# Sliding-window attention and an ELU layer on one core: the score products of a head pair on shared rows

## The chip, the cores and the metric

One core of one Trainium2 chip. The metric is the device time of one execution in microseconds. Three runs of the kernel before took 627.19, 627.75 and 628.57 us; the median is 627.75 us.

## What is computed

Attention over 4 batches, 8 heads, 768 positions and a head dimension of 64, in which a query sees the first 4 keys ("sinks") and the last 128 keys up to its own position; then a layer of 512 -> 2048 -> 512 with an ELU between, on the 3072 rows that come out. All inputs and the output are float32.

```
scores = (q @ k.T) / sqrt(64)
keep   = (key < n_sink) | ((rel >= 0) & (rel < window))     # rel = query - key
a      = softmax(where(keep, scores, -1e9))
x      = (a @ v), heads side by side                        # 3072 x 512
h      = x @ w_in                                           # 512 x 2048
out    = where(h > 0, h, exp(min(h, 0)) - 1) @ w_out        # 2048 x 512
```

## The kernel before

The 3072 rows are 24 tiles of 128 positions, six to a batch. They are worked on in nine chunks of 2, 2, 2, 3, 3, 3, 3, 3 and 3 tiles (`SIZES`). For every chunk there is attention, for 4 head pairs and each tile, and then the layer, for 16 blocks of 128 hidden columns. A tile that is the first of its batch has one block of keys (4 sinks and 128 keys, 132 columns), every other one two blocks (264 columns).

Full precision is had by splitting a float32 operand into two fp16 parts, "hi" and "lo", and summing products of the parts. In the layer (lines 765 and 793) there are three products for each operand pair: hi x hi, hi x lo and lo x hi. The first product of the layer (L765) makes 12 matrix products of 256 or 384 columns a block, the second (L793) three for each tile, of 512 columns. These two lines are most of TensorE's work.

The scores of chunks 0 to 2 (`c < DUP`) are fp32 products of 64 rows: the two heads of a pair lie in rows 0 to 63 and 64 to 127 of one tile, and line 601 issues one product for each, an fp32 product being two instructions. From chunk 3 on the key and query columns of each head are loaded twice, into rows 0 to 63 and again into rows 64 to 127, by `layouts` on the host's side and one load per head (line 523). `split_keys` (line 508) then makes for each head:

- `hi`, by a ScalarE copy to fp16 of all rows (L524),
- `lo` of the keys, all rows, by a VectorE subtraction (L525),
- `lo` of the queries, written over the lower half of `hi`'s query columns (L526).

A product over all 128 rows with these queries as weights hence sums the query's hi and lo parts by itself, and a head's scores take two products: with `hi` (L595) and with `lo` (L596) of the keys. Each head is a task of its own on TensorE, with its own bank of PSUM out of two. VectorE then adds the mask and finds the row's minimum (L616), ScalarE takes the exponential (L618), the probabilities are split into fp16 parts (L668, L669), transposed by a DMA (L687) and multiplied with the values (L701, L706). The value products have 64 columns of weights, head 0 in the left half of the array and head 1 in the right. From chunk 3 on the value products of three tiles are made in one visit.

All instructions are tasks of a planner (`Plan`). A task has an engine, an expected duration, what it depends on, and for TensorE a position in the stream of layer products. `ring` makes the writer of a buffer wait for the users of its former contents; there are two raw key buffers (`kqs`), three split ones (`kq`) and two score banks (`s`). `forward` (line 193) simulates the engines, and each engine's order comes out of it and is then fixed by `keep_order` (line 920). Until 100 us into the plan, small idle products (L882) fill TensorE's holes. `HINTS` (line 891) places branch hints so many tasks before each queue's end. `check_kq` (line 842) loads the keys and queries of chunks 3 to 8 a second time late in the run, to test their range; it takes rows 0 to 63 of one head and 64 to 127 of the other, as two loads.

Of the kernel before, what the change touches and what calls it, by code (L numbers as in the profile page):

```python
# [20 lines left out]
P = 128  # L21
# [28 lines left out]
DUP = 3  # L50
# [18 lines left out]
for _c, _ch in enumerate(CHUNKS):  # L69
    for _p in range(NP):  # L70
        for _e in range(2):
            KQ_OFF[_c, 2 * _p + _e] = KQ_COLS
            if _c >= DUP or _e:
                KQ_COLS += len(key_tiles(_ch)) * KW + len(_ch) * P
KQ_MAX = max(len(key_tiles(c)) * KW + len(c) * P for c in CHUNKS)
KL_MAX = max(len(key_tiles(c)) * KW for c in CHUNKS)
# [289 lines left out]
def fast_path(tc, ctx, first, kq, vx, wt, out, low, spread, numbers, flag):  # L366
# [14 lines left out]
    kqr = rows("kq", [P, KQ_MAX + KL_MAX], F16)  # L381
# [113 lines left out]
    def attention(c):  # L495
# [12 lines left out]
        def split_keys(h):  # L508


            st = kqs[slot("kqs")]
            o, kw = KQ_OFF[c, h], kc + qc
            if c < DUP:
                ld = None
                if (c, h) not in first["kq"]:
                    ld = add("SP", 0.4, lambda: nc.sync.dma_start(st[:, :kw], kq[:, o : o + kw]), lat=dma_us(P * kw * 4) * 1.15)
                users = []
                return st, None, ld, ld, users
            buf = kqr[slot("kq")]
            raw, hi, lo = st[:, :kw], buf[:, :kw], buf[:, KQ_MAX : KQ_MAX + kc]  # L520
            ld = None
            if (c, h) not in first["kq"]:
                ld = add("SP", 0.4, lambda: nc.sync.dma_start(raw, kq[:, o : o + kw]), lat=dma_us(P * kw * 4) * 1.15)
            th = add("ACT", act_us(kw), lambda: nc.scalar.activation(hi, raw, AF.Copy, scale=Q_SCALE), deps=[ld])  # L524
            tk = add("DVE", 0.13 + 0.00108 * kc, lambda: nc.vector.scalar_tensor_tensor(lo, raw[:, :kc], Q_SCALE, hi[:, :kc], ALU.mult, ALU.subtract), deps=[th], slow=1.5)  # L525
            tq = add("DVE", 0.13 + 0.00108 * qc, lambda: nc.vector.scalar_tensor_tensor(hi[D:, kc:], raw[D:, kc:], Q_SCALE, hi[D:, kc:], ALU.mult, ALU.subtract), deps=[th], slow=1.5)  # L526
            users = []
            ring("kqs", [ld or th], [th, tk, tq])
            ring("kq", [th], users)
            return hi, lo, tk, tq, users  # L530
# [39 lines left out]
        for p in range(NP):  # L570
            kqp = [split_keys(2 * p + e) for e in range(2 if c >= DUP else 1)]
# [4 lines left out]
            for g in ts:  # L576
# [13 lines left out]
                def scores(es_, sps=sps, qo=qo, c0=c0, wd=wd, kqp=kqp):  # L590
                    def run():
                        if c >= DUP:
                            hi, lo = kqp[es_[0]][:2]
                            sp, q = sps[es_[0]], hi[:, qo : qo + P]
                            nc.tensor.matmul(sp[:, :wd], q, hi[:, c0 : c0 + wd], start=True, stop=False)  # L595
                            nc.tensor.matmul(sp[:, :wd], q, lo[:, c0 : c0 + wd], start=False, stop=True)  # L596
                            return
                        both = kqp[0][0]
                        for e in es_:
                            r = slice(e * D, (e + 1) * D)  # L600
                            nc.tensor.matmul(sps[e][:, :wd], both[r, qo : qo + P], both[r, c0 : c0 + wd], start=True, stop=True)  # L601
                    return run

                if c >= DUP:
                    scs = [add("PE", 0.225 if nb == 2 else 0.2, scores([e]), deps=kqp[e][2:4], pos=at[k] + 0.01 * e, line=1) for e in range(2)]
                else:
                    scs = [add("PE", 0.65, scores([0, 1]), deps=kqp[0][2:4], pos=at[k], line=1)] * 2
                for kk, sc_ in zip(kqp, scs):
                    kk[4].append(sc_)
                if c < DUP and j == 0:  # L610
                    ring("kqs", [kqp[0][2] or scs[0]], kqp[0][4])
                to_score = -0.125 / (Q_SCALE * Q_SCALE) if c >= DUP else -0.125
                exps, st_users = [], []
                for e in range(2):
                    ee, me = e3[:, e, :wd], mn[:, e : e + 1]
                    red = add("DVE", 0.24 + 0.001 * wd, lambda ee=ee, me=me, sp=sps[e], m=m, wd=wd, to_score=to_score: nc.vector.tensor_tensor_reduce(ee, sp[:, :wd], m[:, :wd], to_score, 3.0e38, ALU.add, ALU.min, me), deps=[scs[e], (None, second_)[t] if t < 2 else rest_])  # L616
                    ring("s", [scs[e]], [red])
# [224 lines left out]
    def check_kq(c, p, k, after):  # L842
        t, n = vm[slot("vm")].rearrange("p a w -> p (a w)"), len(key_tiles(CHUNKS[c])) * KW + SIZES[c] * P

        def both_heads():
            for e in range(2):
                r, o = slice(e * D, (e + 1) * D), KQ_OFF[c, 2 * p + e]
                nc.sync.dma_start(t[r, :n], kq[r, o : o + n])

        ld = add("SP", 0.8, both_heads, deps=[after], lat=2.0 + dma_us(P * n * 4))  # L850
# [6 lines left out]
    for i in range((len(SIZES) - DUP) * NP):  # L857
        check_kq(DUP + i // NP, i % NP, len(SIZES) * NP + i, exps_done[NF * 6 - 4 + 2 * i])
# [32 lines left out]
HINTS = dict(PE=8, ACT=110, DVE=120, SP=50)  # L891
# [50 lines left out]
def general_path(tc, ctx, kq, vx, wt, out, nw):  # L942
# [50 lines left out]
    for b in range(B):  # L993
        x = sb.tile([P, ND, S], F32, name=f"g_x{b}", tag="g_x", bufs=1)
        for h in range(H):
# [3 lines left out]
            for c, ch in enumerate(CHUNKS):  # L999
                kts = key_tiles(ch)  # L1000
                for i, g in enumerate(ch):
# [4 lines left out]
                    r = slice(0, D) if c >= DUP else slice(h % 2 * D, (h % 2 + 1) * D)  # L1006
# [52 lines left out]
def layouts(q, k, v):  # L1059
# [15 lines left out]
    for c, ch in enumerate(CHUNKS):  # L1075
        kts = key_tiles(ch)
        for h in range(H):
            e = h % 2
            o = KQ_OFF[c, h]
            for src, tiles in ((kx, kts), (qT, ch)):  # L1080
                for g in tiles:
                    w = src.shape[4]
                    for r in (0, 1) if c >= DUP else (e,):
                        kq[r * D : (r + 1) * D, o : o + w] = src[g // NT, h, :, g % NT]
# [87 lines left out]
```

## Time and profile before

| | |
|---|---|
| median of three runs | 627.75 us |
| the profiled execution | 628.19 us |
| its span, first to last instruction | 626.3 us |
| TensorE busy with products | 606.1 us |
| TensorE's mean granted clock | 0.991 of full speed |
| DMA moved | 98.24 MB |

The span is counted from the first instruction of the program to the last; what lies around it, 1.9 us, belongs to the time of the execution. Products on TensorE are pipelined: one is on record until its last result is written, while the next has long begun. The time that a product takes from the stream is therefore read from the start of one to the start of the next, not from its duration. A weight load (PEld) overlaps with products.

### The profile page before, as it was taken

What the parts mean: (1) busy time and instruction counts of PE and PEld (TensorE: products, weight loads), DVE (VectorE), ACT (ScalarE), POOL (GpSimd) and SP (SyncE); (2) the same over time, 40 slices, a digit from 0 to 9 for tenths busy, and PEclk for the clock granted to TensorE, in tenths of its full rate; (3) what the DMA queues carried; (4) which work ended last, traced back from release to release, by engine and by line L of the source; (5) the groups of instructions that cost most, each with busy time, mean ns of one, the idle gap of its engine ahead of it and who ended that gap; (6) DMA issues with size and microseconds to landing.
All of it is one profiled execution on the core that took longest, in us unless ns stands there. A gap on an engine that the chain in (4) does not pass through costs nothing.

```text
span 626.3 us, 13397 instructions
## 1 busy us (share of the span) xinstructions
PE 606.1 (97%) x4504; PEld 359.4 (57%) x4504; DVE 462.3 (74%) x1206; ACT 421.2 (67%) x1192; POOL 294.7 (47%) x595
## 2 busy tenths in 40 slices
PE   6997999999999999999999999999999999999995
PEld 4664665667675555555555555555555555555552
DVE  7877677979878786688788988788877887543323
ACT  5887888879878876676667666676767666432221
POOL 4876689875445444344344445334324444222221
PEclk9898999999999999999999999999999999999998
DMA  8698977758656665586456865676655864413101
GB/s 293 210 248 199 298 243 192 209 139 223 145 127 157 162 146 103 94 216 181 125 153 177 230 139 159 130 197 136 166 125 124 209 144 107 115 50 92 55 2 53
DMA packets 122077, 98.24 MB, mean 157 GB/s; under 512 B 98324, under 2 KB 98324, under 8 KB 122004
## 3 DMA queue, kind: packets, MB, share of 16 engines
q1 hardware_dynamic: 122004, 97.34, 60.7%
q8 instruction: 37, 0.61, 0.4%
q14 instruction: 36, 0.29, 0.2%
HBM read 66.38 MB, written 7.34 MB: 118 GB/s over the span
## 4 chain that ended last, share of the span: by engine, by line
PE 91%; POOL 3%; DVE 2%; issue 2%; DMA 1%; ACT 1%; POOLq 0%; ACTq 0%
PE acc L793 39%; PE h L765 38%; PE po L701 5%; PE s L595 2%; PE s L596 2%; PE s L601 2%; POOL w L457 1%; PE h L882 1%; PE acc L636 1%; DMA pt<-pq 1%; DMA vs<-in_vx_dram 1%; PE po L706 1%; PE po L653 0%; DVE pt L334 0%; POOL pq L630 0%
## 5 line engine op out<-in xcount | busy, mean ns | idle before, releaser
L765 PE MATMUL h<-x,w 128*128 128x384 f16 (+1 forms) x1728 | 274.9, 309 | 2.4 <-DVE g L776 2.3
L765 PEld LDWEIGHTS <-w 128*128 128x128 f16 x1728 | 168.3, 98 | 94.8 <-issue 3.2
L786 POOL TENSOR_TENSOR gl<-g,gh 128x384 f16<-128x384 f32 (+1 forms) x144 | 128.7, 894 | 157.3 <-ACT gh L779 134.2
L793 PE MATMUL acc<-w,gh 128*128 128x512 f16 x768 | 192.7, 379 | 1.0 <-POOL w L457 1.0
L773 ACT ACTIVATE g<-h 128x384 f32<-128x384 f32 (+1 forms) x144 | 65.1, 452 | 101.8 <-PE h L765 92.2
L793 PEld LDWEIGHTS <-gh 128*128 128x128 f16 x768 | 72.9, 98 | 69.4 <-issue 0.9
L793 PE MATMUL acc<-w,gl 128*128 128x512 f16 x384 | 109.2, 379 | 0.0
L669 DVE SCALAR_TENSOR_TENSOR pq<-e,st,pq 128x256 f16<-128x256 f32 (+1 forms) x176 | 95.1, 571 | 13.0 <-ACT pq L668 12.7
L618 ACT ACTIVATE e<-e,st 128x264 f32<-128x264 f32 (+1 forms) x192 | 92.9, 484 | 12.2 <-DVE st L616 11.2
L779 ACT ACTIVATE gh<-g 128x384 f16<-128x384 f32 (+1 forms) x144 | 69.3, 481 | 43.2 <-DVE g L776 41.5
L616 DVE CUSTOM_DVE_ANT_0 e<-s,m 128x264 f32<-128x264 f32 (+1 forms) x192 | 71.7, 405 | 26.2 <-PE s L596 19.8
L776 DVE SCALAR_TENSOR_TENSOR g<-g,h 128x384 f32<-128x384 f32 (+1 forms) x144 | 72.8, 506 | 13.2 <-POOL g L775 11.3
L668 ACT ACTIVATE pq<-e,st 128x256 f16<-128x256 f32 (+1 forms) x176 | 77.1, 482 | 5.3 <-DVE st L623 4.1
L775 POOL TENSOR_SCALAR g<-g 128x384 f32<-128x384 f32 (+1 forms) x80 | 41.5, 518 | 80.2 <-ACT g L773 79.8
L775 DVE TENSOR_SCALAR g<-g 128x384 f32<-128x384 f32 (+1 forms) x64 | 26.8, 419 | 65.7 <-ACT g L773 65.4
L793 PEld LDWEIGHTS <-gl 128*128 128x128 f16 x384 | 37.5, 98 | 46.6 <-POOL gl L786 0.9
L524 ACT ACTIVATE kq<-kqs 128x780 f16<-128x780 f32 (+1 forms) x48 | 42.7, 901 | 15.7 <-PE s L596 12.2
L457 POOL TENSOR_TENSOR w<-wv,w 128x256 f16<-128x256 f32 x64 | 49.2, 789 | 5.4 <-ACT w L456 4.7
L622 POOL TENSOR_SCALAR st<-st 128x2 f32<-128x2 f32 x84 | 21.2, 253 | 48.0 <-ACT e L618 44.1
L701 PE MATMUL po<-pt,vh 128*64 128x128 f16 x656 | 35.8, 221 | 2.6 <-DVE x L740 1.9
L618 ACT ACTIVATION_READ_ACCUMULATOR e<-e,st 128x1 f32 x192 | 36.1, 188 | 0.0
L595 PE MATMUL s<-kq 128*128 128x264 f16 (+1 forms) x144 | 34.3, 267 | 0.6 <-ACT x L739 0.6
(92 smaller groups left out, 628.8 us busy)
## 6 DMA issues: line engine op xcount, KB each, us to landing
raw<-in_wt_dram SPq DMA_DIRECT2D x32, 512.0 KB, 4.8
kqs<-in_kq_dram SPq DMA_DIRECT2D x24, 456.0 KB, 3.6
kqs<-in_kq_dram SPq DMA_DIRECT2D x24, 390.0 KB, 3.6
vs<-in_vx_dram SPq DMA_DIRECT2D x28, 256.0 KB, 3.6
out_dram<-wv SPq DMA_DIRECT2D x24, 256.0 KB, 2.6
vm<-in_kq_dram SPq DMA_DIRECT2D x24, 228.0 KB, 3.7
vm<-in_kq_dram SPq DMA_DIRECT2D x24, 195.0 KB, 3.4
vm<-in_vx_dram SPq DMA_DIRECT2D x6, 768.0 KB, 5.3
```

Source lines behind the costliest of these rows:

```text
L616: red = add("DVE", 0.24 + 0.001 * wd, lambda ee=ee, me=me, sp=sps[e], m=m, wd=wd, to_score=to_score: nc.vector.tensor_tensor_reduce(ee, sp ...
L618: ex = add("ACT", 0.47 + 0.00085 * wd, lambda ee=ee, me=me, rs=rs[:, e : e + 1]: nc.scalar.activation(ee, ee, AF.Exp, bias=me, scale=-1.0, ...
L668: a = add("ACT", act_us(nb * P, True), lambda src=src, hi=hi, re=re: nc.scalar.activation(hi, src, AF.Copy, scale=re), deps=[rr])
L669: b = add("DVE", 0.478 if nb == 2 else 0.33, lambda src=src, hi=hi, lo=lo, re=re: nc.vector.scalar_tensor_tensor(lo, src, re, hi, ALU.mult ...
L701: nc.tensor.matmul(po[e * D : (e + 1) * D, oc], vts[i][x][:, vo : vo + D], pt[:, (2 * e + part) * nb + i, :], start=new, stop=last)
L765: nc.tensor.matmul(hp[:, :n], win[:, part, d, :], xx[:, :n], start=k == 0, stop=k == 3 * ND - 1)
L773: a = add("ACT", act_us(n) + 0.18, lambda gf=gf, hp=hp, sums=sums: nc.scalar.activation(gf, hp[:, :n], AF.Exp, scale=1.0 / G_SCALE, accum_ ...
L775: b = add("DVE", 0.14 + 0.00057 * n, lambda gf=gf: nc.vector.tensor_scalar(gf, gf, -1.0, G_SCALE, ALU.add, ALU.mult), deps=[a], slow=2.1, ...
L776: b = add("DVE", dve_us(n), lambda gf=gf, hp=hp: nc.vector.scalar_tensor_tensor(gf, gf, 0.0, hp[:, :n], ALU.min, ALU.max), deps=[b])
L779: th = add("ACT", act_us(n), lambda gf=gf, gh=gh: nc.scalar.activation(gh[:, :n], gf, AF.Copy), deps=[b])
L786: tls.append(add("POOL", pool_us(cut), lambda gl=gl, gf=gf, gh=gh, cut=cut: nc.gpsimd.tensor_tensor(gl[:, :cut], gf[:, :cut], gh[:, :cut], ...
L793: nc.tensor.matmul(acc[i], gg[:, i * P : (i + 1) * P], wout[:, part, :], start=f == f0 and k == 0, stop=f == f1 - 1 and k == 2)
```

## The change

From chunk 3 on the two heads of a pair are no longer loaded twice over all rows; they share one tile as in the first chunks, head 0 in rows 0 to 63 and head 1 in rows 64 to 127. `split_keys` is called once for a pair. `lo` gets a place of its own for the queries too. The scores are three products of 64 rows for each head, hi x hi, hi x lo and lo x hi (query x key), the two heads in turn, and are one task. The product of the two lo parts, which was part of the sum before, is left out. `check_kq` makes one load of 128 rows. Two branch hints move. Cut to its core:

```diff
--- before.py
+++ after.py
...
     for _p in range(NP):
         for _e in range(2):
             KQ_OFF[_c, 2 * _p + _e] = KQ_COLS
-            if _c >= DUP or _e:
+            if _e:
                 KQ_COLS += len(key_tiles(_ch)) * KW + len(_ch) * P
 KQ_MAX = max(len(key_tiles(c)) * KW + len(c) * P for c in CHUNKS)
-KL_MAX = max(len(key_tiles(c)) * KW for c in CHUNKS)
 VT = NP * P
 SINKS = B * NT * VT
 TOK_MAX = max(SIZES) * P
...
 
     kqs = first["kqs"]
     vs = first["vs"]
-    kqr = rows("kq", [P, KQ_MAX + KL_MAX], F16)
+    kqr = rows("kq", [P, 2 * KQ_MAX], F16)
     vh = rows("vh", [P, VT], F16, RINGS["vt"])
     vl = rows("vl", [P, VT], F16, RINGS["vt"])
     sks = rows("sk", [P, VT], F16)
...
                 users = []
                 return st, None, ld, ld, users
             buf = kqr[slot("kq")]
-            raw, hi, lo = st[:, :kw], buf[:, :kw], buf[:, KQ_MAX : KQ_MAX + kc]
+            raw, hi, lo = st[:, :kw], buf[:, :kw], buf[:, KQ_MAX : KQ_MAX + kw]
             ld = None
             if (c, h) not in first["kq"]:
                 ld = add("SP", 0.4, lambda: nc.sync.dma_start(raw, kq[:, o : o + kw]), lat=dma_us(P * kw * 4) * 1.15)
             th = add("ACT", act_us(kw), lambda: nc.scalar.activation(hi, raw, AF.Copy, scale=Q_SCALE), deps=[ld])
-            tk = add("DVE", 0.13 + 0.00108 * kc, lambda: nc.vector.scalar_tensor_tensor(lo, raw[:, :kc], Q_SCALE, hi[:, :kc], ALU.mult, ALU.subtract), deps=[th], slow=1.5)
-            tq = add("DVE", 0.13 + 0.00108 * qc, lambda: nc.vector.scalar_tensor_tensor(hi[D:, kc:], raw[D:, kc:], Q_SCALE, hi[D:, kc:], ALU.mult, ALU.subtract), deps=[th], slow=1.5)
+            tk = add("DVE", 0.13 + 0.00108 * kc, lambda: nc.vector.scalar_tensor_tensor(lo[:, :kc], raw[:, :kc], Q_SCALE, hi[:, :kc], ALU.mult, ALU.subtract), deps=[th], slow=1.5)
+            tq = add("DVE", 0.13 + 0.00108 * qc, lambda: nc.vector.scalar_tensor_tensor(lo[:, kc:], raw[:, kc:], Q_SCALE, hi[:, kc:], ALU.mult, ALU.subtract), deps=[th], slow=1.5)
             users = []
             ring("kqs", [ld or th], [th, tk, tq])
             ring("kq", [th], users)
...
 
         k = 0
         for p in range(NP):
-            kqp = [split_keys(2 * p + e) for e in range(2 if c >= DUP else 1)]
+            kqp = split_keys(2 * p)
 
 
             po = po_ps[slot("po")]
...
                 pq = pqs[slot("pq")]
                 pt = pts[slot("pt")]
 
-                def scores(es_, sps=sps, qo=qo, c0=c0, wd=wd, kqp=kqp):
-                    def run():
-                        if c >= DUP:
-                            hi, lo = kqp[es_[0]][:2]
-                            sp, q = sps[es_[0]], hi[:, qo : qo + P]
-                            nc.tensor.matmul(sp[:, :wd], q, hi[:, c0 : c0 + wd], start=True, stop=False)
-                            nc.tensor.matmul(sp[:, :wd], q, lo[:, c0 : c0 + wd], start=False, stop=True)
-                            return
-                        both = kqp[0][0]
-                        for e in es_:
+                def scores(sps=sps, qo=qo, c0=c0, wd=wd, kqp=kqp):
+                    hi, lo = kqp[:2]
+                    qs, ks = slice(qo, qo + P), slice(c0, c0 + wd)
+                    products = ((hi, hi), (hi, lo), (lo, hi)) if c >= DUP else ((hi, hi),)
+                    for n, (q, k) in enumerate(products):
+                        for e in range(2):
                             r = slice(e * D, (e + 1) * D)
-                            nc.tensor.matmul(sps[e][:, :wd], both[r, qo : qo + P], both[r, c0 : c0 + wd], start=True, stop=True)
-                    return run
-
-                if c >= DUP:
-                    scs = [add("PE", 0.225 if nb == 2 else 0.2, scores([e]), deps=kqp[e][2:4], pos=at[k] + 0.01 * e, line=1) for e in range(2)]
-                else:
-                    scs = [add("PE", 0.65, scores([0, 1]), deps=kqp[0][2:4], pos=at[k], line=1)] * 2
-                for kk, sc_ in zip(kqp, scs):
-                    kk[4].append(sc_)
+                            nc.tensor.matmul(sps[e][:, :wd], q[r, qs], k[r, ks], start=n == 0, stop=n == len(products) - 1)
+
+                sc = add("PE", (0.40 if nb == 2 else 0.30) if c >= DUP else 0.65, scores, deps=kqp[2:4], pos=at[k], line=1)
+                kqp[4].append(sc)
                 if c < DUP and j == 0:
-                    ring("kqs", [kqp[0][2] or scs[0]], kqp[0][4])
+                    ring("kqs", [kqp[2] or sc], kqp[4])
                 to_score = -0.125 / (Q_SCALE * Q_SCALE) if c >= DUP else -0.125
                 exps, st_users = [], []
                 for e in range(2):
                     ee, me = e3[:, e, :wd], mn[:, e : e + 1]
-                    red = add("DVE", 0.24 + 0.001 * wd, lambda ee=ee, me=me, sp=sps[e], m=m, wd=wd, to_score=to_score: nc.vector.tensor_tensor_reduce(ee, sp[:, :wd], m[:, :wd], to_score, 3.0e38, ALU.add, ALU.min, me), deps=[scs[e], (None, second_)[t] if t < 2 else rest_])
-                    ring("s", [scs[e]], [red])
+                    red = add("DVE", 0.24 + 0.001 * wd, lambda ee=ee, me=me, sp=sps[e], m=m, wd=wd, to_score=to_score: nc.vector.tensor_tensor_reduce(ee, sp[:, :wd], m[:, :wd], to_score, 3.0e38, ALU.add, ALU.min, me), deps=[sc, (None, second_)[t] if t < 2 else rest_])
+                    ring("s", [sc], [red])
...
                     exps.append((red, ex))
 
...
     def check_kq(c, p, k, after):
         t, n = vm[slot("vm")].rearrange("p a w -> p (a w)"), len(key_tiles(CHUNKS[c])) * KW + SIZES[c] * P
 
-        def both_heads():
-            for e in range(2):
-                r, o = slice(e * D, (e + 1) * D), KQ_OFF[c, 2 * p + e]
-                nc.sync.dma_start(t[r, :n], kq[r, o : o + n])
-
-        ld = add("SP", 0.8, both_heads, deps=[after], lat=2.0 + dma_us(P * n * 4))
+        o = KQ_OFF[c, 2 * p]
+        ld = add("SP", 0.4, lambda: nc.sync.dma_start(t[:, :n], kq[:, o : o + n]), deps=[after], lat=2.0 + dma_us(P * n * 4))
...
         ring("vm", [ld], new)
         seen.extend(new)
...
     for c in range(len(SIZES)):
         check_v(c, exps_done[NF * 4 + 3 * c])
     for i in range((len(SIZES) - DUP) * NP):
-        check_kq(DUP + i // NP, i % NP, len(SIZES) * NP + i, exps_done[NF * 6 - 4 + 2 * i])
+        check_kq(DUP + i // NP, i % NP, len(SIZES) * NP + i, exps_done[len(exps_done) - 4 - 2 * ((len(SIZES) - DUP) * NP - i)])
 
     def in_range():
         for r, most in ((es_of, EXP_MAX), (v_top, V_MAX)):
...
 VERBOSE = False
 
 
-HINTS = dict(PE=8, ACT=110, DVE=120, SP=50)
+HINTS = dict(PE=8, ACT=90, DVE=120, SP=27)
 E = mybir.EngineType
 QUEUES = dict(PE=E.PE, ACT=E.Activation, DVE=E.DVE, SP=E.SP)
 
...
                         continue
                     j, ts = kts.index(g), slice(g % NT * P, (g % NT + 1) * P)
                     o = KQ_OFF[c, h]
-                    r = slice(0, D) if c >= DUP else slice(h % 2 * D, (h % 2 + 1) * D)
+                    r = slice(h % 2 * D, (h % 2 + 1) * D)
                     nc.sync.dma_start(kt[:, ts], kq[r, o + j * KW + NS : o + (j + 1) * KW])
                     o += len(kts) * KW + i * P
                     nc.sync.dma_start(qt[:, ts], kq[r, o : o + P])
...
             for src, tiles in ((kx, kts), (qT, ch)):
                 for g in tiles:
                     w = src.shape[4]
-                    for r in (0, 1) if c >= DUP else (e,):
-                        kq[r * D : (r + 1) * D, o : o + w] = src[g // NT, h, :, g % NT]
+                    kq[e * D : (e + 1) * D, o : o + w] = src[g // NT, h, :, g % NT]
                     o += w
     return kq, vx
 
```

## Rows read from the trace of the kernel before

**Rows 1.** the page's first part: busy time, share of the span, instructions by engine.

```profile
PE 606.1 (97%) x4504; PEld 359.4 (57%) x4504; DVE 462.3 (74%) x1206; ACT 421.2 (67%) x1192; POOL 294.7 (47%) x595
```

**Rows 2.** the page's fourth part: chain that ended last, shares by engine.

```profile
PE 91%; POOL 3%; DVE 2%; issue 2%; DMA 1%; ACT 1%; POOLq 0%; ACTq 0%
```

**Rows 3.** stretches: length, busy PE, PEld, DVE, ACT, POOL, then PEclk, DMA share, GB/s.

```profile
0.00:120.00 120.00, 106.86 (x826) 69.20 (x827) 91.31 (x260) 96.50 (x269) 88.72 (x183) 0.97 0.82 242
120.00:560.00 440.00, 439.43 (x3362) 259.31 (x3360) 347.05 (x895) 307.53 (x880) 192.06 (x397) 1.00 0.62 148
```

**Rows 4.** waits of PE from 120 us to the end: total us, times, longest.

```profile
PE s L595 <- ACT x L739: 0.6, 1, 0.6
```

**Rows 5.** timeline of PE, a long and a short tile's scores: start us, us.

```profile
300.57 0.28 PE L595 MATMUL s<-kq 128*128 128x264 f16 x1
300.69 0.28 PE L596 MATMUL s<-kq 128*128 128x264 f16 x1
...
301.02 2.11 PE L765 MATMUL h<-x,w 128*128 128x384 f16 x12
302.98 1.46 PE L793 MATMUL acc<-w,gh 128*128 128x512 f16 x6
...
304.92 0.22 PE L595 MATMUL s<-kq 128*128 128x132 f16 x1
...
305.15 2.11 PE L765 MATMUL h<-x,w 128*128 128x384 f16 x12
```

**Rows 6.** score tile: instructions, ns min/median/max, first and last start us, forms.

```profile
L595 PE MATMUL s<-kq x144: 218/276/287, 132.1 to 536.2; 128*128 128x264 f16 x120, 128*128 128x132 f16 x24
L596 PE MATMUL s<-kq x144: 219/276/276, 132.2 to 536.3; 128*128 128x264 f16 x120, 128*128 128x132 f16 x24
L601 PE MATMUL s<-kqs x96: 272/462/806, 5.0 to 110.5; 64*128 64x264 f32 x80, 64*128 64x132 f32 x16
```

**Rows 7.** timeline of PE, a values visit and what stands around it.

```profile
313.38 2.11 PE L765 MATMUL h<-x,w 128*128 128x384 f16 x12
315.43 0.25 PE L701 MATMUL po<-pt,vh 128*64 128x128 f16 x2
315.50 0.22 PE L701 MATMUL po<-pt,vl 128*64 128x128 f16 x2
315.56 0.33 PE L701 MATMUL po<-pt,vh 128*64 128x128 f16 x6
315.73 0.28 PE L701 MATMUL po<-pt,vl 128*64 128x128 f16 x4
...
316.29 0.22 PE L706 MATMUL po<-pt,sk 128*64 128x128 f16 x2
316.44 1.47 PE L793 MATMUL acc<-w,gh 128*128 128x512 f16 x6
```

**Rows 8.** timeline of PE in narrow stretches, the fp32 scores at 91.6 us.

```profile
91.09 0.59 PE L793 MATMUL acc<-w,gl 128*128 128x512 f16 x2
91.62 0.49 PE L601 MATMUL s<-kqs 64*128 64x264 f32 x2
91.94 0.39 PE L601 MATMUL s<-kqs 64*128 64x264 f32 x2
92.26 0.50 PE L765 MATMUL h<-x,w 128*128 128x256 f16 x3
```

**Rows 9.** timeline of PE, scores right behind a values visit.

```profile
427.15 0.22 PE L706 MATMUL po<-pt,sk 128*64 128x128 f16 x2
427.30 0.29 PE L595 MATMUL s<-kq 128*128 128x264 f16 x1
```

**Rows 10.** the page's fifth part: count, busy us, mean ns, idle before, releaser.

```profile
L616 DVE CUSTOM_DVE_ANT_0 e<-s,m 128x264 f32<-128x264 f32 (+1 forms) x192 | 71.7, 405 | 26.2 <-PE s L596 19.8
...
L524 ACT ACTIVATE kq<-kqs 128x780 f16<-128x780 f32 (+1 forms) x48 | 42.7, 901 | 15.7 <-PE s L596 12.2
```

**Rows 11.** timeline of PEld, a weight load of the scores.

```profile
300.58 0.10 PEld L596 LDWEIGHTS <-kq 128*128 128x128 f16 x1
```

## The prediction

> **What bounds the kernel now.** I read the share of each engine first: TensorE 97%, the next engine 74% [rows 1]. The chain of work that ended last says the same, 91% of the span on TensorE [rows 2]. Then I asked where TensorE still has room. Between 120 and 560 us, where all of the changed products lie, it is busy for all but 0.6 us, at a granted clock of 1.00, the 2.4 GHz level; the only wait in the list from there on is one of 0.6 us. Before 120 us some 13 us stand without a product [rows 3, 4]. The scores of chunks 3 to 8, the ones the change rewrites, are four products of 128 rows per tile of a head pair. They slot into the stream without a gap: from 300.57 to 301.02 for 264 columns, 0.45 us, and from 304.92 to 305.15 for 132 columns, 0.23 us [rows 5]. So one long product is 0.1125 us and one short one 0.0575 us. The two lines of the code have 120 long and 24 short instructions each [rows 6]: 60 long and 12 short tiles of a pair, 29.8 us of TensorE. So only what the change does to TensorE's own stream can move the time; work taken off the other engines has no waiting product to release.
>
> **Part 1, the products.** Four products of 128 rows become three rounds of two 64-row products, the heads in different halves of the array. If the halves run together a round takes what one product takes: 3 x 0.1125 = 0.34 us long, 3 x 0.0575 = 0.17 short. That they can is shown by the fp32 scores of the first chunks, which have this very form: two 64-row instructions, 0.46 us the median of one, are over in 0.49 us together [rows 6, 8]. I add 0.01 us for the lag of the second head. In columns alone, this saves 60 x 0.1125 + 12 x 0.0575 = 7.4 us.
>
> **Part 2, entering and leaving the split array.** The trace shows no fp16 64-row product, so its price comes from two neighbours. The nearest in type is the fp16 values visit, which splits the array by columns. Twelve layer products take 1.96 us when more full-array products follow (301.02 to 302.98) and 2.05 us when a visit follows (313.38 to 315.43): 0.09 us to enter [rows 5, 7]. The first pair is followed by the next after 0.07 us, later pairs after 0.055 (315.56 to 315.73 for three): about 0.02 for weights that nothing hides. Leaving, the last pair at 316.29 is followed by a layer product at 316.44: 0.15 instead of 0.055, so 0.095 us; the six products behind it then take 1.47 instead of 1.46, another 0.01 [rows 5, 7]. Together 0.215, say 0.22 us per visit.
>
> The nearest in form is the fp32 score at 91.6 us. Two layer products from 91.09 would end at 91.52 (0.215 each); the scores begin at 91.62, again 0.09 to 0.10 later. Its last round at 91.94 is followed at 92.26, 0.32 later. If 0.095 of that is leaving, a round is 0.225, just twice the fp16 product of the same width. The first round, 91.62 to 91.94, then holds 0.10 of weight loading, and the whole passage costs 0.74 - 0.45 = 0.29 us over its columns [rows 8]. The same gap of 0.09 stands in rows of both kinds of split, so I take it for a cost of the split and not of the type. For the weights I take the fp16 price: 0.22 a passage. The upper end is 0.29. The lower end, the two empty stretches alone, is 0.185; below that only the case that no such stretch occurs, a rival below.
>
> Per tile of a pair: long, 0.22 + 0.01 + 0.34 = 0.57 against 0.45, **+0.12 us**; short, 0.22 + 0.01 + 0.17 = 0.40 against 0.23, **+0.17 us**. That is 60 x 0.1175 + 12 x 0.1725 = 9.1 us. Where scores stand beside a values visit one entry is shared: such neighbours occur six times in the timeline from 120 us on, and I quote one [rows 9]; 6 x 0.1 = 0.6 us back. Sum **+8.5 us**.
>
> **Part 3, the splitting of keys and queries.** One load, one ScalarE copy and two VectorE subtractions per head become one each per pair: 24 fewer of each kind, and 24 fewer loads on SyncE's queue with half the bytes. ScalarE loses half of 42.7 us of copies [rows 10]; the subtractions of VectorE are of the same number. I cost all of it at nothing: both engines already wait for TensorE at this place (the copy 12.2 us in all, the score reduction 19.8 us) [rows 10], while TensorE waits 0.6 us. On SyncE's queue the transposes and loads behind get more room, which again nobody on TensorE is waiting for. If the splits are what that one wait hangs on, the 0.6 us is all there is to win; and as the work shrinks, nothing that it covers is laid open.
>
> **Part 4, both heads in one task.** The six products wait for both score banks and both subtractions, where each head waited for its own before. Behind them on TensorE stand the layer products. VectorE waits for these scores rather than the other way (19.8 us) and the next tile comes 4 us later (300.57, 304.92) [rows 5, 10], so I take nothing. A missed bank would cost up to one reduction, 0.41 us [rows 10]; a few such would be within my range. The first reduction starts some 0.3 us later; its engine has that room.
>
> **Part 5, order and end.** The planner is told 0.40 and 0.30 us for scores it used to count at 0.45 and 0.40, and fewer tasks elsewhere; every queue's order may shift. From 120 to 560 us nothing waits, so that is free; before 120 us, 13 us stand open [rows 3], but the first of the changed scores comes at 132.1 us [rows 6]; a different order of the work ahead could give or take perhaps a tenth, 1.3 us either way. The range checks of the keys become one load of 128 rows instead of two of 64, the same bytes; their trigger works out to the same place in the list of exponentials. The branch hints move, for ScalarE and SyncE only; the trace doesn't show their price, bounded by the 1.9 us around the span (628.19 - 626.3) as gain or loss; I take nothing, as the last products and stores are the same.
>
> **The sum.** The profiled execution took 628.19 us, 0.44 over the median of 627.75. 628.2 + 8.5 = 636.7 in its terms, **636.3 us** as a median. A measurement here can tell about 0.2%, 1.3 us, from no change.
>
> **Rivals.** (A) *Faster: fp16 halves of rows need no emptying of the array.* The drains in fp32 would then belong to fp32 and those of the visits to columns. The time is 628.2 - 7.4 + 72 x 0.01 = 621.5, median 621.1. The point from which it decides: below 0.09 us a passage the change gains. For it: no row shows the new form. Against: fp32 scores and fp16 visits, different in type and in split, show the same 0.09 on entering. The Trainium skill (TensorEngine Tiling (Array Packing), Theoretical Speedup) promises up to twice the speed for a dimension of 64 or less, which by itself gives this rival's time. The same page (Key Properties) says that changing the tiling mode drains the engine, and the two gaps in the rows agree with that.
>
> (B) *The heads take turns.* An fp32 round takes twice the time for the same columns (0.225 against 0.1125), so the halves may share something that fp16 at full rate exhausts. Three more rounds a tile: 60 x 0.34 + 12 x 0.17 = 22.4 us more, 658.7. Against it: the fp16 visits run their pairs together, 0.055 a pair where a product of 132 columns takes 0.0575 [rows 5, 7].
>
> (C) *Weights wait for their own rows.* If a head's next weights could not be loaded while its half streams, rounds two and three would each show a load, 0.10 us by the row of one [rows 11]: 72 x 2 x 0.10 = 14.4 us more, 650.7. Against it: with all 128 rows in use, the load at 300.58 lies inside the product that started at 300.57, and the next starts at 300.69 without a gap [rows 5, 11]; and in fp32 the second round shows no further gap. The Trainium skill (TensorE: Matmul & The Clock Gate, Part 3, The mechanism) says that a weight load overlaps a running product only where the row groups differ, which would give this rival's time; the rows of the full array contradict it as it stands there.
>
> (D) *No net change:* passages at about 0.09 us, half-hidden, 627 to 629.
>
> **Chances.** Forecast 0.78, A 0.10, B 0.05, C 0.04, D 0.03. The number is the forecast's. The range takes the overhead from 0.185 (-2.5 us) to 0.29 (+5.0), the shared entries from none to twice six (0.6 either way) and 1.3 us either way for the order: 636.3 - 4.4 is 631.9 with all three, 636.3 + 5.6 is 641.9 with the first two; I give 631.5 to 642, leaving out A, B, C and D, about 0.2. Faster 0.10 (A), same 0.03 (D), slower 0.87.
>
> **What would show it.** Right: score instructions on 64 rows, two starting together, rounds 0.11 us apart; about 0.09 us between the last layer product's normal end and the first score, and again behind it; a long tile taking 0.57 us of the stream; TensorE still without waits from 120 us; the key copy's count at 24 and its wait gone, with no effect on time. Wrong: a layer product following the third round at 0.11 us (A), six evenly spaced starts (B), rounds at 0.21 us (C), or new waits of TensorE for score banks or keys (part 4).

## The result, and the profile after

The kernel after took 634.64 us (median of four runs, 634.41 to 636.12) against 627.48 us before (four runs as well, one more than the three given above): 1.0116 times as long, with an interval of 1.0096 to 1.0136. That is 7.2 us slower, where 8.5 were forecast; 634.64 lies within the range. The profiled execution took 636.12 us, the longest of the four.

The page's first part and its fourth, of the kernel after, to be held against [rows 1] and [rows 2]:

```profile
PE 613.3 (97%) x4648; PEld 342.0 (54%) x4648; DVE 434.0 (68%) x1164; ACT 404.6 (64%) x1164; POOL 287.9 (45%) x593
...
PE 91%; POOL 4%; DMA 2%; DVE 1%; ACT 1%; issue 1%; SPq 0%; ACTq 0%; POOLq 0%
```

VectorE has 28 us less to do and ScalarE 17, as the change has it, and the time grew all the same: TensorE is still at 97% and holds 91% of the chain. From 120 us to the end the list of TensorE's waits has no entry at all, and the stretches (columns as in [rows 3]) show it busy throughout:

```profile
120.00:560.00 440.00, 440.00 (x3472) 239.09 (x3471) 317.10 (x851) 290.01 (x848) 185.12 (x395) 1.00 0.53 126
```

So the list shows no wait for another engine that could be the loss. The loss stands in the stream of products, and the timeline shows where. One long tile and one short tile of the kernel after; the rows of one and two instructions come from narrow stretches around their starts:

```profile
303.87 0.59 PE L783 MATMUL acc<-w,gl 128*128 128x512 f16 x2
304.39 0.29 PE L596 MATMUL s<-kq 64*128 64x264 f16 x2
304.52 0.39 PE L596 MATMUL s<-kq 64*128 64x264 f16 x4
304.84 0.50 PE L755 MATMUL h<-x,w 128*128 128x384 f16 x2
...
308.53 0.38 PE L783 MATMUL acc<-w,gl 128*128 128x512 f16 x1
308.84 0.23 PE L596 MATMUL s<-kq 64*128 64x132 f16 x2
...
309.12 2.12 PE L755 MATMUL h<-x,w 128*128 128x384 f16 x12
```

The two layer products that start at 303.87 would be done with the stream at 304.30 (0.215 each: six are on record for 1.46 us [rows 5] and one for 0.38); the scores start at 304.39. The first two score instructions take 0.29 us together, from the start of the one to the end of the other, where one alone takes 0.28: they run side by side. The second round starts 0.13 later at 304.52, and the next layer product at 304.84, 0.32 after the second round. Two rounds at 0.1125 are 0.225 of that, and the rest, 0.095, is a gap in which no product starts. The long tile takes 304.84 - 304.30 = 0.54 us of the stream, against 0.45 before [rows 5] and 0.57 forecast. The short one takes 309.12 - 308.75 = 0.37, against 0.23 and 0.40.

The groups of other engines that answer to [rows 10]:

```profile
L606 DVE CUSTOM_DVE_ANT_0 e<-s,m 128x264 f32<-128x264 f32 (+1 forms) x192 | 71.6, 406 | 50.4 <-PE s L596 48.0
...
L523 ACT ACTIVATE kq<-kqs 128x780 f16<-128x780 f32 (+1 forms) x24 | 21.7, 905 | 17.4 <-PE s L596 17.4
```

The copies went from 48 to 24, and work that was saved turned into longer waits for TensorE: 48.0 us in front of the score reduction instead of 19.8, 17.4 in front of half as many copies instead of 12.2.

### The profile page after: what moved, and what is told of

Read it like the earlier page. It is cut to its first block, busy times and chain, and to the rows that moved or that the text cites. A ratio compares the mean times of both kernels' runs of the same rounds, so it can differ in the third digit from the quotient of the medians.

```text
span 634.3 us, 13457 instructions
## 1 busy us (share of the span) xinstructions
PE 613.3 (97%) x4648; PEld 342.0 (54%) x4648; DVE 434.0 (68%) x1164; ACT 404.6 (64%) x1164; POOL 287.9 (45%) x593
## 4 chain that ended last, share of the span: by engine, by line
PE 91%; POOL 4%; DMA 2%; DVE 1%; ACT 1%; issue 1%; SPq 0%; ACTq 0%; POOLq 0%
PE acc L783 39%; PE h L755 39%; PE s L596 6%; PE po L691 5%; POOL w L456 2%; DMA raw<-in_wt_dram 2%; PE po L696 1%; PE h L868 1%; POOL pq L620 1%; DVE pt L333 0%; ACT wu L306 0%; POOL gl L776 0%; ACT pq L658 0%; ACT g L763 0%; DVE pq L659 0%
## 5 line engine op out<-in xcount | busy, mean ns | idle before, releaser
L755 PEld LDWEIGHTS <-w 128*128 128x128 f16 x1728 | 164.8, 98 | 103.4 <-issue 10.4
L776 POOL TENSOR_TENSOR gl<-g,gh 128x384 f16<-128x384 f32 (+1 forms) x144 | 126.2, 877 | 170.1 <-ACT gh L769 140.9
L783 PEld LDWEIGHTS <-gh 128*128 128x128 f16 x768 | 71.1, 98 | 74.5 <-issue 6.6
L765 DVE TENSOR_SCALAR g<-g 128x384 f32<-128x384 f32 (+1 forms) x70 | 28.4, 405 | 69.4 <-ACT g L763 69.3
L765 POOL TENSOR_SCALAR g<-g 128x384 f32<-128x384 f32 (+1 forms) x74 | 37.2, 503 | 59.0 <-ACT g L763 58.5
L596 PE MATMUL s<-kq 64*128 64x264 f16 (+1 forms) x432 | 34.8, 267 | 0.0
L691 PEld LDWEIGHTS <-vh 128*64 128x64 f16 x656 | 26.6, 111 | 13.7 <-issue 13.6
```

The source lines that it names most:

```text
L596: nc.tensor.matmul(sps[e][:, :wd], q[r, qs], k[r, ks], start=n == 0, stop=n == len(products) - 1)
L691: nc.tensor.matmul(po[e * D : (e + 1) * D, oc], vts[i][x][:, vo : vo + D], pt[:, (2 * e + part) * nb + i, :], start=new, stop=last)
L755: nc.tensor.matmul(hp[:, :n], win[:, part, d, :], xx[:, :n], start=k == 0, stop=k == 3 * ND - 1)
L765: b = add("DVE", 0.14 + 0.00057 * n, lambda gf=gf: nc.vector.tensor_scalar(gf, gf, -1.0, G_SCALE, ALU.add, ALU.mult), deps=[a], slow=2.1, ...
L776: tls.append(add("POOL", pool_us(cut), lambda gl=gl, gf=gf, gh=gh, cut=cut: nc.gpsimd.tensor_tensor(gl[:, :cut], gf[:, :cut], gh[:, :cut], ...
L783: nc.tensor.matmul(acc[i], gg[:, i * P : (i + 1) * P], wout[:, part, :], start=f == f0 and k == 0, stop=f == f1 - 1 and k == 2)
```

## The experiments

To keep the start out of the comparison I also read one stretch in every trace: from the first product of the layer's second half for chunk 3 (the fourth chunk) to that for chunk 7, four chunks of work. In it lie 48 score tiles of head pairs, 40 long and 8 short, and 16 values visits; the layer's products are the same in every kernel. Its length in the kernel before, from the two products that bound it in the timeline of TensorE (line numbers move with the edits):

```profile
202.96 1.24 PE L793 MATMUL acc<-w,gh 128*128 128x512 f16 x5
...
492.08 1.24 PE L793 MATMUL acc<-w,gh 128*128 128x512 f16 x5
```

The same two products in the kernel after:

```profile
205.11 1.25 PE L783 MATMUL acc<-w,gh 128*128 128x512 f16 x5
...
499.37 1.25 PE L783 MATMUL acc<-w,gh 128*128 128x512 f16 x5
```

289.12 us became 294.26: 5.14 us for 48 tiles, 0.107 us a tile. Seventy-two such tiles make 7.7 us, about the whole of what was measured.

The theory was that each passage into and out of the split array costs about 0.21 us and outweighs the columns saved. Its rivals: that the loss comes from the shared task, the order or the start; that the halves do not run together; and that the work taken off the other engines matters after all.

### No split at all

```diff
+                    if c >= DUP:
+                        for e, k, first_, last_ in ((0, hi, True, False), (0, lo, False, True), (1, hi, True, True)):
+                            nc.tensor.matmul(sps[e][:, :wd], hi[:, qs], k[:, ks], start=first_, stop=last_)
+                        return
                     for n, (q, k) in enumerate(products):
```

> The kernel after, but from chunk 3 on a tile's scores are three products over all 128 rows (two into head 0's bank, one into head 1's), so the array is never split for them. The columns streamed, the task, the order and all other engines' work stay as after; the scores are sums over both heads and so not the reference's. Theory (the passages into and out of the split array cost about 0.21 us a tile, more than the columns saved): 72 x 0.21 = 15 us less than after, 619.5 us (618.5 to 621). Rival (the loss comes from the one task for both heads, from the order or from the work at the start): no passage was to be paid for, so it stays within 2 us of after's 634.6.

Measured: 620.72 us, 0.9895 times before (0.9880 to 0.9911), 13.9 us less than after. The tile in the stream and the bounds of the stretch:

```profile
200.32 1.24 PE L787 MATMUL acc<-w,gh 128*128 128x512 f16 x5
...
484.14 0.50 PE L595 MATMUL s<-kq 128*128 128x264 f16 x3
484.48 1.24 PE L787 MATMUL acc<-w,gh 128*128 128x512 f16 x5
```

Three products take 484.48 - 484.14 = 0.34 us and the layer follows without a gap. The stretch is 284.16 us long. Against before it is 4.96 us shorter; the columns saved are 40 x 0.1125 + 8 x 0.0575 = 4.96 us. Against after it is 10.10 us shorter: 0.210 us for each of the 48 passages (one of them lies right behind a values visit and shares an entry with it). The task, the order's rules and the other engines are those of after, so the rival falls: without the split, the same kernel would be faster than before. It is no version to keep, since its scores mix the heads.

### Two passages instead of one

```diff
                             nc.tensor.matmul(sps[e][:, :wd], q[r, qs], k[r, ks], start=n == 0, stop=n == len(products) - 1)
+                        if c >= DUP and n == 0:
+                            nc.tensor.matmul(sps[0][:, 300:304], hot[:, :P], hot[:, :4], start=False, stop=False)
```

> The kernel after with one full-array product of 4 columns (into unused columns of head 0's bank) between the first and the second round of each tile, which makes two passages of one; the scores stay the same. Theory (each passage empties the array twice): 72 x (0.095 + 0.03 + 0.095 + about 0.02 for weights) = 17 us more than after, 652 us (649 to 654). Rival (the cost is paid once per tile, whatever happens inside, for instance for the wait on both heads): 4 columns alone, 72 x 0.03 = 2 us more, 637 us.

Measured: 650.26 us, 1.0362 times before (1.0344 to 1.0380), 15.6 us more than after. Its timeline of TensorE, the bounds of the stretch and the tile ahead of the second:

```profile
207.64 1.25 PE L785 MATMUL acc<-w,gh 128*128 128x512 f16 x5
...
511.65 0.29 PE L596 MATMUL s<-kq 64*128 64x264 f16 x2
511.87 0.18 PE L598 MATMUL s<-hot 128*128 128x4 bf16 x1
511.98 0.40 PE L596 MATMUL s<-kq 64*128 64x264 f16 x4
512.31 1.25 PE L785 MATMUL acc<-w,gh 128*128 128x512 f16 x5
```

The small product waits until 511.87, 0.22 after the first round began, though that round needs 0.1125; and the second round starts 0.11 behind a product of 4 columns. That leaves at most 0.02 for the 4 columns themselves; the 0.03 in the expectation was not read from any run, and with it the 17 us came out a little high. The stretch grew by 304.67 - 294.26 = 10.41 us, 0.217 us for each passage added. With the experiment above, one kernel with a passage less and one with a passage more give the same price.

### Head 0's products first, then head 1's

```diff
-                    for n, (q, k) in enumerate(products):
-                        for e in range(2):
+                    for e in range(2):
+                        for n, (q, k) in enumerate(products):
                             r = slice(e * D, (e + 1) * D)
```

> The kernel after with head 0's three products first and then head 1's, not alternating. Theory (products start in program order, a half takes one at a time, and the halves overlap only where neighbours in the program lie in different halves): only head 0's last and head 1's first overlap, five rounds instead of three: 60 x 0.225 + 12 x 0.115 = 15 us more than after, 649.5 us (648 to 651). Rival 1 (each half works off its own list): the same as after, 634.6 us. Rival 2 (the halves take turns in after as well): six rounds in both, so the same as after.

Measured: 635.04 us, 1.0121 times before (1.0097 to 1.0146): the theory's 649.5 was wrong. A tile in the stream:

```profile
303.05 0.38 PE L783 MATMUL acc<-w,gl 128*128 128x512 f16 x1
303.36 0.29 PE L596 MATMUL s<-kq 64*128 64x264 f16 x2
...
303.81 2.12 PE L755 MATMUL h<-x,w 128*128 128x384 f16 x12
```

The bounds of the stretch:

```profile
203.98 1.25 PE L783 MATMUL acc<-w,gh 128*128 128x512 f16 x5
...
498.56 1.25 PE L783 MATMUL acc<-w,gh 128*128 128x512 f16 x5
```

Within 0.29 us two instructions have started and ended, though the program has three of one head before the first of the other. The six still take three rounds: 303.36 to 303.81 is 0.45, as in after (304.39 to 304.84), and the stretch is 294.58 us, 0.32 more than after for 48 tiles. Either each half works off its own products without waiting for its turn in the program, or the halves matter in neither kernel. The next experiment tells these apart.

### All six products in one half

```diff
-                            r = slice(e * D, (e + 1) * D)
+                            r = slice(0, D) if c >= DUP else slice(e * D, (e + 1) * D)
```

> The kernel after with both heads' products from chunk 3 on taken from rows 0 to 63, so that all six lie in one half of the array; head 1's scores are head 0's. Theory (a half takes one product at a time, the two halves run together in after): six rounds instead of three, 60 x 0.34 + 12 x 0.17 = 22.4 us more than after, 657 us (655 to 658). Rival (the six products are not bound by the half they lie in): 634.6 us.

Measured: 656.74 us, 1.0462 times before (1.0446 to 1.0477); 657 was expected. Its timeline of TensorE, the bounds of the stretch and the tile ahead of the second, and below it the weight loads of that tile:

```profile
208.90 1.25 PE L783 MATMUL acc<-w,gh 128*128 128x512 f16 x5
...
517.11 0.85 PE L596 MATMUL s<-kq 64*128 64x264 f16 x6
517.88 1.25 PE L783 MATMUL acc<-w,gh 128*128 128x512 f16 x5
...
517.10 0.56 PEld L596 LDWEIGHTS <-kq 64*128 64x128 f16 x6 [0.32 <-issue]
```

The six take 0.77 us to the next layer product instead of 0.45. The stretch is 308.98 us, 14.72 more than after; three more rounds are 40 x 0.3375 + 8 x 0.1725 = 14.9. So a half takes one product at a time and the two halves do run together in after. With it, the experiment before has one reading left: a product of the half that is free starts ahead of products of the busy half that stand before it in the program. (The records do not name the half; that the first two lie in different halves follows, since one half takes one product at a time.) Alternating, as the change has it, is not needed for that. This run also speaks against a load of weights that must wait for its half: 0.77 us holds six rounds of 0.1125, each with its load, and the 0.095 of leaving, and no more.

### Half of the splits, in the kernel before

```diff
-            kqp = [split_keys(2 * p + e) for e in range(2 if c >= DUP else 1)]
+            kqp = [split_keys(2 * p)] * (2 if c >= DUP else 1)
```

> The kernel before, but head 1 of each pair from chunk 3 on uses head 0's split keys and queries, so that 24 loads, 24 ScalarE copies and 48 VectorE subtractions fall away, as many as in the change; TensorE's products are those of before, head 1's scores are head 0's. Theory (that work was hidden behind TensorE): the same as before, 627.5 us, within 0.8 us. Rival (it was on the path): some us less, down to 625.

Measured: 628.97 us (eight runs), 1.0023 times before (1.0012 to 1.0033): slower by 1.7 us in the medians, with less work, which neither theory had. The bounds of the stretch in its timeline:

```profile
204.31 1.24 PE L793 MATMUL acc<-w,gh 128*128 128x512 f16 x5
...
493.43 1.24 PE L793 MATMUL acc<-w,gh 128*128 128x512 f16 x5
```

The stretch is 289.12 us, to the hundredth that of before. So in this stretch, which holds 48 of the 72 tiles, loads, copies and subtractions are worth nothing, as forecast. The loss was there before the stretch began, 204.31 instead of 202.96. With fewer tasks the planner makes another order for all queues. From 120 us on one new kind of wait shows, two scores that waited for the reduction of earlier ones to free their bank (the list of TensorE's waits: us in all, times, longest):

```profile
PE s L595 <- DVE st L616: 0.6, 2, 0.3
```

They do not carry the loss: before has 0.6 us of waiting there too, in one wait for ScalarE [rows 4], and that one is gone. Whether the 1.7 us come from the new order or from another effect of the missing work was not tried.

### Scores beside the values visits

```diff
-V_AT = 7
+V_AT = 8
```

> The kernel after with the value visits asked for one position later (V_AT = 8), which puts a tile's scores right beside the visit in 25 places of TensorE's order instead of 5. Theory (going from one kind of split to the other empties the array once, where leaving and entering empty it twice): 20 x 0.095 = 1.9 us less than after, 632.7 us, give or take 1 us for the order at the start. Rival (the emptying is paid at each end of each kind, beside or not): the same as after, 634.6 us, give or take as much.

Measured: 633.42 us (six runs, 631.35 to 636.31), 1.0094 times before (1.0071 to 1.0117). The median is 1.2 us under that of after, which the spread of the runs does not bear out by itself. The trace does. The bounds of the stretch, and one of the places inside:

```profile
204.80 1.24 PE L783 MATMUL acc<-w,gh 128*128 128x512 f16 x5
...
319.50 0.22 PE L696 MATMUL po<-pt,sk 128*64 128x128 f16 x2
319.66 0.51 PE L596 MATMUL s<-kq 64*128 64x264 f16 x6
320.10 1.47 PE L783 MATMUL acc<-w,gh 128*128 128x512 f16 x6
...
497.45 1.24 PE L783 MATMUL acc<-w,gh 128*128 128x512 f16 x5
```

From visit to score is 319.66 - 319.50 = 0.16 us, a pair's 0.055 and one gap of about 0.1. The stretch is 292.65 us, 1.61 less than after, with 16 such neighbours instead of 1: 0.107 us for each entry that is shared.

### A planner told the true durations, and the old hints

```diff
-                sc = add("PE", (0.40 if nb == 2 else 0.30) if c >= DUP else 0.65, scores, deps=kqp[2:4], pos=at[k], line=1)
+                sc = add("PE", (0.54 if nb == 2 else 0.38) if c >= DUP else 0.65, scores, deps=kqp[2:4], pos=at[k], line=1)
```

> The kernel after, its planner told 0.54 and 0.38 us for the scores, about what the trace of after shows, instead of 0.40 and 0.30. Nothing but the order of the tasks can change. Theory (from 120 us on TensorE never waits, so the order is free there, and the start may give or take 1 us): 634.6 us, within 1.2 us. Rival (a good part of the 7 us is a bad order, made from wrong durations): 632 us or less.

```diff
-HINTS = dict(PE=8, ACT=90, DVE=120, SP=27)
+HINTS = dict(PE=8, ACT=110, DVE=120, SP=50)
```

> The kernel after with the branch hints of before. Theory (the hints' place costs nothing here): 634.6 us, within 0.7 us. Rival (they are worth up to the 1.9 us around the span): 633 or 636.5 us.

Measured: 636.03 us (633.66 to 636.46), 1.0124 times before (1.0107 to 1.0142), and 635.83 us (633.65 to 636.09), 1.0115 times before (1.0099 to 1.0132). Both medians lie above the bounds I had given the theory, by 0.2 and 0.5 us. The runs of before beside them were at 627.71, though, and by the ratios both stand where after stands with its 1.0116. The bounds of the stretch, first with the true durations, then with the old hints:

```profile
204.88 1.25 PE L783 MATMUL acc<-w,gh 128*128 128x512 f16 x5
...
499.25 1.25 PE L783 MATMUL acc<-w,gh 128*128 128x512 f16 x5
...
204.82 1.04 PE L783 MATMUL acc<-w,gh 128*128 128x512 f16 x4
...
499.08 1.04 PE L783 MATMUL acc<-w,gh 128*128 128x512 f16 x4
```

The stretch is 294.37 and 294.26 us, where after has 294.26; the 0.11 more is about one shared entry, since the order made from the true durations has no score beside a visit there and after's has one. Neither kernel is faster: the rival that an order made from wrong durations is a good part of the loss falls. The runs of either kernel lie 2.4 to 2.8 us apart, more than I had allowed for, so a price of the hints under a microsecond or so stays open.

## Why the prediction was right

**What bounds the kernel.** Right: work off the other engines left TensorE's stretch at 289.12 us, and only its own stream moved the time.

**Part 1, the columns.** Right to the hundredth: 4.96 us saved in the stretch, by the kernel that never splits. The 7.4 for all 72 tiles is the same sum carried on; between the medians 6.5 us show (620.72 and 627.23), with the start in them.

**Part 2, the passages.** The mechanism was right, and the term was a little too large. I took 0.22 for the passage and 0.01 for the lag, 0.23 together; measured are 0.210 (no split against one) and 0.217 (two against one, with its 4 columns). In the stretch, where the start plays no part, the forecast's prices give 40 x 0.1175 + 8 x 0.1725 - 0.1 = 6.0 us, and 5.14 were measured. Over 72 tiles 0.02 is 1.4 us, about what lies between the forecast of 8.5 and the 7.2 measured; that the whole kernel comes this close is partly luck, since its start alone can differ by a microsecond (part 5). The choice between the ends is what mattered: of the fp32 scores' 0.29 and the fp16 visits' 0.22 the nearer was the row of the same type, not the one of the same form. Leaving showed a gap of 0.095 as in both. The shared entry, priced at 0.1, came to 0.107; I had counted six such places, and the new order has five.

The Trainium skill (TensorEngine Tiling (Array Packing), Key Properties) says that a change of the tiling mode drains the engine, and the two experiments that take a passage away and add one fit that, at 0.21 us for in and out.

What the engine does in the gap is less certain than its price. The loads of the weights give another reading. Here are the first load of the long tile above, then all loads of the fp16 scores in after, of the visits in before and of the fp32 scores in before (ns: shortest, median, longest):

```profile
304.39 0.09 PEld L596 LDWEIGHTS <-kq 64*128 64x128 f16 x1 [0.42 <-issue]
...
L596 PEld LDWEIGHTS <-kq x432: 92/94/97, 133.5 to 544.1; 64*128 64x128 f16 x144
...
L701 PEld LDWEIGHTS <-vh x656: 106/110/110, 44.0 to 551.2; 128*64 128x64 f16 x164
...
L601 PEld LDWEIGHTS s<-kqs x96: 182/186/335, 5.0 to 110.3; 64*128 64x128 f32 x96
```

The first load behind a change does not run ahead, as loads inside a stream do [rows 11]: it starts with its product, at 304.39. And the price of entering goes with its length: gap and delay of the second round together are 0.09 and 0.01 to 0.02 for the fp16 scores, 0.09 and 0.02 for the visits, 0.10 and 0.10 for the fp32 scores, where a load takes 0.09, 0.11 and 0.19. So the gap may be an array that runs empty, or a first load that nothing hides; in no run do the two come apart, and which it is stays open. It would explain, though, why the fp32 scores were the wrong neighbour: their loads take twice as long.

**Part 3, the splits.** Right on the path (289.12 us in the stretch), and the one wait of 0.6 us [rows 4], all that part 3 allowed to be won, is gone in the kernel after. "Nothing" was too simple for the whole: with the work gone the kernel before took 1.7 us more, for a reason that was not found. One of the signs named for a right forecast did not come: the wait in front of the key copies did not go but grew, from 12.2 to 17.4 us, since ScalarE has less to do and waits for TensorE the longer.

**Part 4, one task for both heads.** Right: no wait of TensorE for a bank or a key from 120 us on. A wait as short as the gap could not show in that list, since the product ahead is still on record when the scores start (303.87 + 0.59 = 304.46 against 304.39). But the kernel without a split has the same task with the same conditions and no gap, so the gap is no such wait.

**Part 5, order and start.** I allowed 1.3 us either way. In its profiled execution the kernel after is 2.15 us behind before when the stretch begins (205.11 and 202.96). Most of that, 1.4 us, stands ahead of the first passage that the change adds: the first of the changed scores starts at 133.5 us, against 132.1 before [rows 6]. With head 0's products first the order of tasks is that of after, and there the first of them starts at 132.3 us and the stretch begins at 203.98, so about a microsecond differs from one execution to the next. The traces differ in TensorE's granted clock early on (columns as in [rows 3]; after, then head 0 first; below them the scores of each):

```profile
60.00:80.00 20.00, 18.61 (x138) 12.12 (x139) 14.97 (x41) 17.46 (x49) 13.38 (x24) 0.91 0.91 263
60.00:80.00 20.00, 18.44 (x144) 12.02 (x144) 14.65 (x39) 17.47 (x51) 13.74 (x25) 1.00 1.01 280
...
L596 PE MATMUL s<-kq x432: 217/273/284, 133.5 to 544.2; 64*128 64x264 f16 x120, 64*128 64x132 f16 x24
L596 PE MATMUL s<-kq x432: 217/273/284, 132.3 to 543.4; 64*128 64x264 f16 x120, 64*128 64x132 f16 x24
```

From 60 to 80 us after had a mean clock of 0.91, so part of that stretch at the lower level of 1.2 GHz, and shows 138 products there instead of 144. That the clock makes the whole difference is not shown, and what the changed order alone costs or gives at the start was not settled.

**The rivals.** A falls twice: the gaps are there, and taking them away gives the time that A promised, 620.7 for 621.1. B has its price confirmed, 656.7 for 658.7, by the kernel that does put all six in one half; the change does not. C falls with the same run, whose rounds follow each other at 0.1125 us in one half. On it the Trainium skill (TensorE: Matmul & The Clock Gate, Part 3, The mechanism) says that a load overlaps a running product only where the row groups differ; the rounds in one half, each with its load, show no such limit. D falls by the measured ratio, 1.0096 to 1.0136, and by the 0.21 us of a passage, more than twice the 0.09 that it needed.

**A version that beats both.** None was found or tried; these are estimates from the numbers above. In split form a long tile beside a visit costs 0.34 + 0.21 - 0.107 = 0.44 us against 0.45 in full rows, which is no gain to build on. Two long tiles in one passage would take 2 x 0.34 + 0.21 = 0.89 against 0.90, and want four score banks where there are two.

## What to carry to other kernels

Splitting the array saves columns and pays at each change between split and whole, here 0.21 us for going in and coming out, about two products of 264 columns. A split form pays only where one visit saves more than that; this one saved a single product per visit. When TensorE never waits, price a change by starts in its own stream, and count work saved elsewhere as nothing until a wait of TensorE can be named that it ends. Compare traces in a stretch of mid-kernel with the same products in both: here it gave a price per tile to the hundredth, while the starts of single executions differed by a microsecond.

## What the runs showed of the hardware

TensorE ran the two halves as if each had a list of its own: with head 0's three products ahead of head 1's in the program, the six took 0.45 us of the stream, the same as alternating, where one half alone takes 0.77. The Trainium skill (TensorE: Matmul & The Clock Gate, Part 3, The mechanism) says that products keep the program's order in start and end; across two halves the measured time does not allow that, since in that order no fewer than five rounds would follow.

Going from one kind of split straight to the other costs one gap, as going from whole to split does: 0.16 us from the last pair of a visit to the first scores, 0.055 of it the pair.
